# Float32 scores in the first two attention units, and VectorE takes five of eight low parts in the second MoE

## The chip, the cores and the metric

One core of a Trainium2 chip runs the whole program in one launch. The metric is the device time of that launch in microseconds (us). TensorE (PE, with its weight loads as PEld), VectorE (DVE), ScalarE (ACT), GpSimd (POOL) and SyncE (SP, which here issues every DMA) run side by side, each through its own instructions in order, and meet only at semaphores.

## The reference, cut to what matters

```python
def _attn_ref(q, k, v, tau):          # q, k, v: (4, 8, 576, 64), float32
    scores = scale * np.matmul(q, k.transpose(0, 1, 3, 2))
    thresh = np.max(scores, axis=-1, keepdims=True) - tau
    scores = np.where(scores >= thresh, scores, -1000000000.0)
    attn = np.exp(scores - np.max(scores, axis=-1, keepdims=True))
    attn = attn / (np.sum(attn, axis=-1, keepdims=True) + 1e-09)
    return np.matmul(attn, v)

def _moe_ref(x, w_in, w_out):         # x: (2304, 512), w_in: (512, 2048), w_out: (2048, 512)
    h = x @ w_in
    return (h * np.clip(h + 3.0, 0.0, 6.0) / 6.0) @ w_out

def _moe2_ref(x, w_in, w_out):
    h = x @ w_in
    return (h * (1.0 / (1.0 + np.exp(-1.702 * h)))) @ w_out

# x = attention, heads side by side; x = _moe_ref(x); result = _moe2_ref(x)
```

## The kernel before

**Products.** A float32 operand is written as a high part, rounded to the type float32r, and a low part, the rest. A product is then two or three float32r matmuls (high times high, high times low, low times high) that add up in PSUM. Nearly every operand so costs a copy on ACT, which makes the high part, and a subtraction on POOL or DVE, which makes the low part.

**Attention.** There are 16 units of two heads (function `unit`, numbers `u` from 0, four for each batch). For each head SP loads k and q from DRAM, where the host has put each of them twice, on rows 0 to 63 and again on rows 64 to 127. ACT copies k to `kh` and POOL subtracts to get `kl`; POOL scales q by 0.125, ACT copies it to `qs`, and POOL replaces rows 64 to 127 of `qs` by q's low part (L489 to L496). One matmul over 128 rows then gives (high of q + low of q) times `kh`, and a second one the same times `kl`: two for each half of the 576 keys, so four float32r matmuls of 288 columns for a score tile of 128 queries (L518 to L520). A unit has nine score tiles; the middle one holds the last 64 queries of both heads and takes two groups, so a unit has ten groups of four. Behind a score tile come DVE's maximum (`nm`, L529) and threshold, ACT's Exp (L531), DVE's mask with the sum (L532), the transposes on PE (L580), their copies to `eh`, and the product with v (L643 in the first four units, which use float32 there). Two PSUM buffers (`ps`) hold score tiles.

**First MoE.** Weights come as words of 64 bits and are decoded on ACT, DVE and POOL (`decode`, L397 to L399 on DVE); 16 weight tiles are decoded while the first units run. The first MoE of a batch starts when its four units have been turned into x (`moe_a`, L708 and L728), and fills PE between the later units.

**Second MoE** (from about 740 us of the span). Tokens go in five blocks (four of 512, one of 256), the hidden units in two halves, and each half in four pairs of 128 units: 10 blocks of 8 gated units, 80 in all. `hidden2` makes a pair's two sums in PSUM (L865) and brings them to `c` with DVE additions and ACT copies; `gate2` then does, for each of the two: sigmoid on ACT (`tc`, L846), product on DVE (`tc<-tc,c`), high part `g` on ACT, low part `g` on POOL (L849, in the trace at the helper's line L346). `yout` multiplies both parts with the output weights (L728, into `py`).

**What sets the order.** Every instruction is an operation of a plan with a cost and a due time. `Plan.settle` orders all of it by a list schedule (a forward pass by priority and backward passes that make the priorities anew) and the program is emitted in that order. A change of one cost or engine so moves many rows. The plan keeps names listed in `PORT` from running on DVE and POOL together; the low parts of a gate (`GL`) stand there for both engines.

Of the kernel before, what the change touches and what calls it, by code (L numbers as in the profile page):

```python
# [15 lines left out]
ALU = mybir.AluOpType  # L16
# [226 lines left out]
def tile_top_attention_moe_moe2(  # L243
# [21 lines left out]
    CH = [(0, 256), (256, 320)]  # L265
    FULL = 4
    scale = 0.125
# [59 lines left out]
    def pe(n):  # L327
        return 7 + 0.43 * n
# [10 lines left out]
    def pool2(n):  # L339
        return 149 + 2.1 * n  # L340
# [122 lines left out]
    def unit(u, b, j, t0):  # L463

        early = u < FULL
        slots, pad = [(0, 0), (1, 0), None, (0, 1), (1, 1)], 64
# [9 lines left out]
        for hd in range(2):  # L478
            h, q0 = 2 * j + hd, pad * hd
            s0 = min(n for n, t in enumerate(tiles) if t is None or t[0] == hd)  # L480
            kr, qr = (buf("qk", 3, "raw", [P, S]) for _ in range(2))
            khb, klb, qsb = (buf(x, 3, "st", [P, n], F32R) for x, n in (("kh", S), ("kl", S), ("qs", S + pad)))
            kh.append(khb), kl.append(klb), qs.append(qsb)
            cols = slice(q0, q0 + S)
            move(K("ld", s0), "ldk", 4 * P * S, lambda kr=kr, h=h: nc.sync.dma_start(out=kr.t, in_=k2[b, h]), [], [kr])

            for o, i, n in ((0, 256, 64), (64, 0, 256), (320, 320, 256)) if b == 0 and hd else ((0, 0, S),):
                move(K("ld", s0), "ldq", 4 * P * n, lambda qr=qr, h=h, o=o, i=i, n=n: nc.sync.dma_start(out=qr.t[:, o:o + n], in_=q2[b, h, :, i:i + n]), [], [(qr, o)])
# [21 lines left out]
        def score(s):  # L510
# [5 lines left out]

            def mm(hd, q0, st, sp):
                for w, a, z in ((kh, st, False), (kl, False, sp)):  # L518
                    for i in range(2):
                        nc.tensor.matmul(ps.t[:, i, :SH], qs[hd].t[:, q0:q0 + P], w[hd].t[:, i * SH:(i + 1) * SH], start=a, stop=z)  # L520

            for hd in range(2) if t is None else t[:1]:
                q0 = t[1] * P + 2 * pad * hd if t else 0 if hd else 512
                add(PE, 4 * pe(SH), K("S", s), "S", lambda hd=hd, q0=q0: mm(hd, q0, t is not None or hd == 0, t is not None or hd == 1), [qs[hd], kh[hd], kl[hd]], [ps])

# [312 lines left out]

    def gate2(c, T, K):
        t = buf("tc", 2, "ct", [P, 512])  # L840
# [11 lines left out]
    def hidden2(n, w, xs, whole, K):  # L852

# [27 lines left out]
        if whole:  # L881
# [4 lines left out]
            plus(b, first(b), bd, p1, 0)  # L886
            return [gate2(c, T, K) for c in (a, b)]
        p5, u2, bb = buf("p5", 1, "ct", [P, 256]), buf("u2", 1, "ct", [P, 256]), bank(3)
# [11 lines left out]
        add(ACT, act(n), K("H2") + 5000, "KP", copy(first(b), first(ba)), [ba], [(b, 0)])  # L900
        return [gate2(c, T, K) for c in (a, b)]

    def moe2(c0, T, f0, w, t0, last):
# [18 lines left out]
        for i in range(len(w)):  # L922
            g2 = hidden2(n, w[i], xs, whole, lambda name, i=i: K(name, i))
            if i:
                yout(i - 1, gs)
            gs = g2
        yout(len(w) - 1, gs)
        for c in range(KC):
# [15 lines left out]
            else:  # L944
# [116 lines left out]
```

## Time and profile before

| | us |
|---|---|
| median of 3 runs | 1147.12 (1145.11 to 1147.84) |
| the profiled execution | 1150.94 |
| its span, first to last instruction | 1149.2 |
| PE busy in it | 1094.7 (95%) |
| DVE / ACT / POOL busy in it | 785.2 / 705.1 / 705.3 |
| mean granted TensorE clock | 0.994 |

A matmul counts as busy until its result has drained, so a PE that is busy 95% of the time is not one that streams columns 95% of the time; how dense it is shows in the starts of its instructions. The difference between the profiled execution and the median is that of single executions, and sums are made against the profiled one.

### The profile page before, as it was taken

Reading aid. Unit: us, or ns where it says so; the run is one execution under the profiler, and the core shown is the slowest. Engines: PE = TensorE matmul, PEld = TensorE weight load, DVE = VectorE, ACT = ScalarE, POOL = GpSimd, SP = SyncE. Lnnn points to the kernel's source line nnn. Section 1 sums busy time; section 2 is a strip of 40 time slices with the busy share of each in tenths; the row PEclk is TensorE's granted clock in tenths of the full one; section 3 lists DMA queues with packets and bytes.
Section 4 is the critical chain, followed back from the end, with each engine's and each line's share of the span. In section 5 each row is a group of like instructions: output and inputs, shape, how many; then the busy total and the mean of one; then the engine's idle time right before and its main releaser. Section 6 shows DMA issues by size and latency. Waiting matters only on the chain.

```text
span 1149.2 us, 21102 instructions
## 1 busy us (share of the span) xinstructions
PE 1094.7 (95%) x7560; PEld 1005.9 (88%) x7560; DVE 785.2 (68%) x1596; ACT 705.1 (61%) x1452; POOL 705.3 (61%) x738
## 2 busy tenths in 40 slices
PE   4999999999999999999899999989999999999998
PEld 3655799989999999999899999988888888889788
DVE  5978886989599959767876432686677865543423
ACT  6877976778678867666554333655556565444432
POOL 6768898878688976556566224675564665432421
PEclk9999999999999999999999999999999999999999
DMA  6434322222222220145664312432544435312202
GB/s 187 149 114 128 98 63 68 75 76 74 67 77 79 69 67 28 48 148 165 194 185 133 98 55 71 152 110 77 172 132 166 157 114 166 111 37 74 88 1 69
DMA packets 79752, 119.00 MB, mean 104 GB/s; under 512 B 7840, under 2 KB 50464, under 8 KB 79648
## 3 DMA queue, kind: packets, MB, share of 16 engines
q1 hardware_dynamic: 79648, 117.67, 33.3%
q8 instruction: 59, 0.97, 0.4%
q14 instruction: 45, 0.37, 0.1%
HBM read 87.10 MB, written 30.54 MB: 102 GB/s over the span
## 4 chain that ended last, share of the span: by engine, by line
PE 60%; DVE 14%; issue 9%; POOL 7%; ACT 6%; DMA 5%; SPq 0%; POOLq 0%; DVEq 0%; ACTq 0%
PE py L728 15%; PE pm L708 14%; PE pm L865 8%; PE pm L728 5%; PE ps L520 5%; PE pm L580 5%; PE pm L643 4%; DVE nm L529 2%; POOL g L346 2%; PE pm L645 2%; DVE e L532 2%; PE pm L647 1%; DVE tc L346 1%; DVE el L346 1%; DVE outlring L346 1%
## 5 line engine op out<-in xcount | busy, mean ns | idle before, releaser
L728 PE MATMUL py<-g,outhring 128*128 128x512 f32 (+2 forms) x1152 | 291.2, 338 | 12.0 <-POOL g L346 8.5
L728 PEld LDWEIGHTS py<-g,outhring 128*128 128x128 f32 x1152 | 193.7, 188 | 35.1 <-POOL g L346 14.1
L346 POOL TENSOR_TENSOR g<-tc,g 128x512 fp32r<-128x512 f32 (+1 forms) x80 | 101.5, 1273 | 158.9 <-ACT g L343 136.9
L728 PE MATMUL py<-g,outlring 128*128 128x512 f32 (+2 forms) x576 | 193.6, 336 | 0.0
L865 PE MATMUL pm<-outhring,inhring 128*128 128x256 f32 x512 | 146.0, 285 | 8.6 <-ACT p L343 4.1
L708 PE MATMUL pm<-xh,inhring 128*128 128x256 f32 (+1 forms) x512 | 153.2, 299 | 0.8 <-DVE t L720 0.3
L708 PE MATMUL pm<-xl,inhring 128*128 128x256 f32 (+1 forms) x512 | 151.2, 295 | 0.0
L708 PE MATMUL pm<-xh,inlring 128*128 128x256 f32 (+1 forms) x512 | 151.0, 295 | 0.0
L865 PE MATMUL pm<-outlring,inhring 128*128 128x256 f32 x512 | 144.0, 281 | 0.0
L865 PE MATMUL pm<-outhring,inlring 128*128 128x256 f32 x512 | 143.8, 281 | 0.0
L346 POOL TENSOR_TENSOR g<-t,g 128x256 fp32r<-128x256 f32 (+1 forms) x104 | 85.7, 828 | 92.2 <-ACT g L343 89.3
L529 DVE TENSOR_REDUCE nm<-ps 128x1 f32<-128x576 f32 x144 | 107.7, 752 | 24.1 <-PE ps L520 23.0
L720 DVE SCALAR_TENSOR_TENSOR t<-t,pm 128x256 f32<-128x256 f32 (+1 forms) x128 | 57.3, 450 | 93.8 <-ACT t L719 93.3
L343 ACT ACTIVATE eh<-pm 128x512 fp32r<-128x512 f32 (+9 forms) x240 | 108.2, 486 | 19.7 <-PE pm L580 18.3
L728 PEld LDWEIGHTS py<-g,outlring 128*128 128x128 f32 x576 | 108.2, 188 | 9.8
L728 PE MATMUL pm<-g,outhring 128*128 128x256 f32 (+1 forms) x512 | 109.4, 303 | 2.1 <-DVE g L346 1.0
L865 PEld LDWEIGHTS pm<-outhring,inhring 128*128 128x128 f32 x512 | 96.8, 189 | 15.4 <-ACT p L343 5.3
L719 ACT ACTIVATE t<-pm,half 128x256 f32<-128x256 f32 (+1 forms) x128 | 63.6, 497 | 75.9 <-PE pm L708 70.0
L531 ACT ACTIVATE e<-ps,nm 128x576 f32<-128x576 f32 x128 | 93.8, 738 | 22.9 <-DVE nm L529 20.1
L532 DVE SCALAR_TENSOR_TENSOR e<-ps,th,e 128x576 f32<-128x576 f32 x128 | 103.0, 811 | 6.4 <-ACT e L531 4.9
L580 PE MATMUL pm<-id,e 128*128 128x128 f32 (+1 forms) x640 | 98.2, 278 | 7.7 <-DVE e L532 7.1
L865 PEld LDWEIGHTS pm<-outlring,inhring 128*128 128x128 f32 x512 | 97.0, 189 | 2.7
(115 smaller groups left out, 2856.1 us busy)
## 6 DMA issues: line engine op xcount, KB each, us to landing
qk<-in_k_dram SPq DMA_DIRECT2D x32, 288.0 KB, 2.9
wrawstg<-in_w1i_dram SPq DMA_DIRECT2D x16, 512.0 KB, 3.8
wrawstg<-in_w1o_dram SPq DMA_DIRECT2D x16, 512.0 KB, 3.5
wrawstg<-in_w2i_dram SPq DMA_DIRECT2D x16, 512.0 KB, 3.8
wrawstg<-in_w2o_dram SPq DMA_DIRECT2D x16, 512.0 KB, 3.7
qk<-in_q_dram SPq DMA_DIRECT2D x28, 288.0 KB, 2.8
wrawstg<-kept SPq DMA_DIRECT2D x20, 256.0 KB, 3.7
xa<-x2d SPq DMA_DIRECT2D x8, 512.0 KB, 3.8
```

The costliest lines, as they stand in the source:

```text
L343: return lambda: nc.scalar.activation(out=o(), in_=i(), func=ACTF.Copy, **kw)
L346: return lambda: (nc.vector if eng == DVE else nc.gpsimd).tensor_tensor(out=o(), in0=a(), in1=b(), op=op)
L520: nc.tensor.matmul(ps.t[:, i, :SH], qs[hd].t[:, q0:q0 + P], w[hd].t[:, i * SH:(i + 1) * SH], start=a, stop=z)
L529: add(DVE, 665, K("R", s), "R", lambda: nc.vector.tensor_reduce(out=nm.t[:, c], in_=ps.t[:, :, :SH], op=ALU.max, axis=AX.XY, negate=True), ...
L531: add(ACT, 624, K("X", s), "X", lambda: nc.scalar.activation(out=ev(), in_=ps.t[:, :, :SH], func=ACTF.Exp, bias=nm.t[:, c]), [ps, (nm, s)] ...
L532: add(DVE, 729, K("M", s), "M", lambda: nc.vector.scalar_tensor_tensor(out=ev(), in0=ps.t[:, :, :SH], scalar=th.t[:, c], in1=ev(), op0=ALU ...
L580: nc.tensor.transpose(pt.t[:kn, o + m * P:o + (m + 1) * P], e_of[s].t[:, ks], id_b.t)
L708: nc.tensor.matmul(ph.t[:, :n], a, v, start=(cc == 0 and i == 0), stop=(cc == KC - 1 and i == 2))
L719: add(ACT, 93 + act(n), K("RL"), "RL", lambda: nc.scalar.activation(out=tt_(), in_=pt(), func=ACTF.Relu, scale=1.0 / 6.0, bias=half_b.t), ...
L720: add(DVE, dve(n), K("GT"), "GT", lambda: nc.vector.scalar_tensor_tensor(out=tt_(), in0=tt_(), scalar=1.0, in1=pt(), op0=ALU.min, op1=ALU. ...
L728: nc.tensor.matmul(py.t[:, :n], a, v, start=(st and i == 0), stop=(sp and i == 2))
L865: nc.tensor.matmul(o.t[:, :n], u.t[:, ws], v.t[:, xv], start=(st and kk == 0 and i == 0), stop=(sp and kk == 1 and i == 2), skip_group_che ...
```

## The change

In units 0 and 1 (`EXACT = 2`) the score operands stay float32: q and k are loaded on rows 0 to 63 only, straight into `qs` and `kh`, POOL fills the other rows with zeros, and DVE scales q in place. The four float32r matmuls of a group become two float32 matmuls. The copies to `kh` and `qs`, the subtractions for `kl` and q's low part and POOL's scaling go away for these four heads. In the second MoE DVE, not POOL, makes the low part of the second gated unit of each pair, and of both units of the last pair of a block: 50 of 80.

```diff
-    FULL = 4
+    FULL, EXACT = 4, 2
...
+            pieces = ((0, 256, 64), (64, 0, 256), (320, 320, 256)) if b == 0 and hd else ((0, 0, S),)
+            if exact:
+                add(POOL, 124 + 0.52 * (S + pad), K("qz", s0), "qz", lambda qsb=qsb: nc.gpsimd.memset(f32(qsb.t)[64:], 0.0), [], [(qsb, 1)])
+                add(POOL, 100, K("qz", s0), "qz", lambda qsb=qsb, z=(1 - hd) * S: nc.gpsimd.memset(f32(qsb.t)[:64, z:z + pad], 0.0), [], [(qsb, 2)])
+                add(POOL, 124 + 0.52 * S, K("qz", s0), "qz", lambda khb=khb: nc.gpsimd.memset(f32(khb.t)[64:], 0.0), [], [(khb, 1)])
+                for o, i, n in pieces:
+                    move(K("ld", s0), "ldq", 256 * n, lambda qsb=qsb, h=h, o=q0 + o, i=i, n=n: nc.sync.dma_start(out=f32(qsb.t)[:64, o:o + n], in_=q2[b, h, :64, i:i + n]), [], [(qsb, o)])
+                move(K("ld", s0), "ldk", 256 * S, lambda khb=khb, h=h: nc.sync.dma_start(out=f32(khb.t)[:64], in_=k2[b, h, :64]), [], [(khb, 0)])
+                for o, i, n in pieces:
+                    add(DVE, 69 + 0.521 * n, K("qs", s0), "qs",
+                        lambda qsb=qsb, c=slice(q0 + o, q0 + o + n): nc.vector.tensor_scalar(out=f32(qsb.t)[:64, c], in0=f32(qsb.t)[:64, c], scalar1=sc_b.t[:64], scalar2=1.0, op0=ALU.mult, op1=ALU.mult), [sc_b], [(qsb, o)])
+                continue
...
             def mm(hd, q0, st, sp):
+                if exact:
+                    for i in range(2):
+                        nc.tensor.matmul(ps.t[:, i, :SH], f32(qs[hd].t)[:, q0:q0 + P], f32(kh[hd].t)[:, i * SH:(i + 1) * SH], start=st, stop=sp)
+                    return
...
-        add(POOL, pool2(T), K("GL2"), "GL", tt(POOL, v(gl), v(t), lambda: f32(v(gh)()), ALU.subtract), [t, gh], [gl])
+        add(eng, pool2(T) if eng == POOL else dve(T), K("GL2"), "GL", tt(eng, v(gl), v(t), lambda: f32(v(gh)()), ALU.subtract), [t, gh], [gl])
...
-            g2 = hidden2(n, w[i], xs, whole, lambda name, i=i: K(name, i))
+            g2 = hidden2(n, w[i], xs, whole, lambda name, i=i: K(name, i), (DVE, DVE) if i == len(w) - 1 else (POOL, DVE))
```

How the order moves is shown at three places.

POOL at the start of the program, before the change, from behind the first fills (`kl` and the second `qs` are the low parts of k and q, `qk` is raw k or q):

```order
L496 MEMSET qs 128x64
L365 MEMSET two 64x64 x2
L346 ISA
L346 TENSOR_TENSOR kl<-qk,kh 128x576
L492 TENSOR_SCALAR qk<-qk,sc 128x576
L346 TENSOR_TENSOR kl<-qk,kh 128x576
L346 TENSOR_TENSOR qs<-qk,qs 64x576
L346 TENSOR_TENSOR id_107<-id 128x64
```

The same place of the changed program:

```order
L488 MEMSET qs 64x640
L489 MEMSET qs 64x64
L490 MEMSET kh 64x576
L488 MEMSET qs 64x640
L489 MEMSET qs 64x64
L490 MEMSET kh 64x576
L365 MEMSET two 128x128
```

Four long operations that the first scores need have gone from POOL; fills of zeros, which wait for no load, stand there instead.

PE at the start, before (`ps` score tiles, `pm<-id,e` transposes, `pm<-eh,vs` products with v; a group of four score matmuls is two rows `kh` and two rows `kl` of a half each, printed as pairs):

```order
L520 MATMUL ps<-kh,qs 128x288 x2
L520 MATMUL ps<-kl,qs 128x288 x2
L520 MATMUL ps<-kh,qs 128x288 x2
L520 MATMUL ps<-kl,qs 128x288 x2
L580 MATMUL pm<-id,e 128x128 x8
L580 MATMUL pm<-id,e 64x128 x2
L520 MATMUL ps<-kh,qs 128x288 x2
L520 MATMUL ps<-kl,qs 128x288 x2
```

And in the changed program:

```order
L535 MATMUL ps<-kh,qs 128x288 x6
L599 MATMUL pm<-id,e 128x128 x8
L599 MATMUL pm<-id,e 64x128 x2
L535 MATMUL ps<-kh,qs 128x288 x2
L662 MATMUL pm<-eh,vs 64x256 x5
```

A score group is one row of two matmuls, and three groups, no longer two, stand ahead of the first transposes.

DVE at the end of the last block of 512 tokens in the second MoE, before (`c` the sums, `tc` the gate, `yc` the output):

```order
L346 TENSOR_TENSOR c<-pm,p_14137 128x256
L346 TENSOR_TENSOR c<-pm,u_14189 128x256
L346 TENSOR_TENSOR c<-pm,p_14147 128x256
L346 TENSOR_TENSOR tc<-tc,c 128x512 x2
L346 TENSOR_TENSOR yc<-py_13982,yc 128x512
```

And in the changed program:

```order
L346 TENSOR_TENSOR c<-pm,u_14119 128x256
L346 TENSOR_TENSOR g<-tc,g 128x512
L346 TENSOR_TENSOR tc<-tc,c 128x512
L346 TENSOR_TENSOR g<-tc,g 128x512
L346 TENSOR_TENSOR c<-pm,p_14098 128x256
L346 TENSOR_TENSOR tc<-tc,c 128x512
L346 TENSOR_TENSOR g<-tc,g 128x512
L346 TENSOR_TENSOR yc<-py_13924,yc 128x512
```

The low parts `g<-tc,g` now stand between the products and the sums on DVE; the sums and the outputs queue behind them.

## Rows read from the trace of the kernel before

**Rows 1.** The head of the page.

```profile
span 1149.2 us, 21102 instructions
```

**Rows 2.** Windows: stretch, length; busy us PE, PEld, DVE, ACT, POOL; clock; DMA.

```profile
10.46:65.00 54.54, 48.55 (x258) 34.05 (x258) 46.12 (x104) 45.51 (x89) 40.46 (x47) 0.97 0.47 141
...
740.00:1149.00 409.00, 388.47 (x2478) 346.69 (x2476) 238.31 (x358) 209.23 (x436) 197.26 (x149) 1.00 0.33 106
```

**Rows 3.** Timeline, start to first MoE matmul: start, length, instruction, idle before.

```profile
0.72 0.38 SPq L485 DMA_DIRECT2D qk<-in_k_dram  x1
...
2.09 0.43 SPq L485 DMA_DIRECT2D qk<-in_k_dram  x1
...
3.60 0.68 ACT L343 ACTIVATE kh<-qk 128x576 fp32r<-128x576 f32 x1 [1.61 <-DMA qk<-in_k_dram]
...
6.77 0.68 ACT L343 ACTIVATE kh<-qk 128x576 fp32r<-128x576 f32 x1 [2.49 <-DMA qk<-in_k_dram]
...
9.01 1.39 POOL L346 TENSOR_TENSOR qs<-qk,qs 64x576 fp32r<-64x576 f32 x1
...
10.46 0.85 PE L520 MATMUL ps<-kh,qs 128*128 128x288 f32 x2 [10.46 <-POOL qs L346]
...
124.07 0.28 PE L708 MATMUL pm<-xh,inhring 128*128 128x256 f32 x1
```

**Rows 4.** Timeline of PE alone: float32r pairs, then float32 products (two records each).

```profile
23.19 0.43 PE L520 MATMUL ps<-kh,qs 128*128 128x288 f32 x2
23.45 0.42 PE L520 MATMUL ps<-kl,qs 128*128 128x288 f32 x2
...
34.17 1.83 PE L643 MATMUL pm<-eh,vs 128*64 128x320 f32 x6
...
39.79 1.29 PE L643 MATMUL pm<-eh,vs 128*64 128x320 f32 x4
```

**Rows 5.** Waits of 10 to 124 us: us in total, times, longest.

```profile
DVE nm L529 <- PE ps L520: 16.2, 18, 2.5
```

**Rows 6.** The chain that ended last, 10 to 60 us, by line.

```profile
by line: PE pm L643 35.0%; PE ps L520 28.4%; PE pm L580 18.8%; DVE nm L529 5.9%; issue 4.2%; DVE e L532 3.6%; POOL qs L346 2.8%; DVE th L530 1.2%; PE pm L571 0.9%; DVE wmstg L397 0.7%; DVE er L532 0.5%; DVE rc L539 0.2%; DVE wmstg L399 0.1%
```

**Rows 7.** Groups by form, 10.46 to 65 us: busy us, mean ns, idle before.

```profile
L397 DVE TENSOR_SCALAR wmstg<-wmstg 128x512 f32<-128x512 f32 x6 | 5.0, 834 | 6.7 <-ACT wmstg L396 6.7
...
L346 POOL TENSOR_TENSOR qs<-qk,qs 64x576 fp32r<-64x576 f32 x5 | 7.1, 1428 | 1.7 <-ACT qs L343 1.3
L346 POOL TENSOR_TENSOR kl<-qk,kh 128x576 fp32r<-128x576 f32 x5 | 7.1, 1420 | 1.1 <-ACT kh L343 1.0
L492 POOL TENSOR_SCALAR qk<-qk,sc 128x576 f32<-128x576 f32 x6 | 4.8, 805 | 4.1 <-DMA qk<-in_q_dram 4.0
```

**Rows 8.** Waits of PE, 740 to 1149 us.

```profile
PE py L728 <- POOL g L346: 8.5, 13, 1.6
...
PE pm L865 <- DVE c L346: 2.3, 4, 1.0
```

**Rows 9.** Groups by form, 740 to 1149 us.

```profile
L346 DVE TENSOR_TENSOR tc<-tc,c 128x512 f32<-128x512 f32 x64 | 60.1, 939 | 38.5 <-ACT tc L846 37.8
...
L346 POOL TENSOR_TENSOR g<-tc,g 128x512 fp32r<-128x512 f32 x64 | 88.6, 1386 | 133.7 <-ACT g L343 111.8 <-issue 9.3 <-PE pm L865 6.4
```

**Rows 10.** DVE on the tile tc, 740 to 1149 us: ns min/median/max.

```profile
L346 DVE TENSOR_TENSOR tc<-tc,c x80: 410/692/1808, 742.4 to 1140.9; 128x512 f32<-128x512 f32 x64, 128x256 f32<-128x256 f32 x16
```

**Rows 11.** Timeline at the end of a block of the second MoE.

```profile
1069.30 1.31 POOL L346 TENSOR_TENSOR outlring<-xb,outhring 128x512 fp32r<-128x512 f32 x1 [0.55 <-ACT outhring L343]
...
1069.55 1.61 DVE L346 TENSOR_TENSOR tc<-tc,c 128x512 f32<-128x512 f32 x1
...
1075.56 1.30 POOL L346 TENSOR_TENSOR outlring<-xa,outhring 128x512 fp32r<-128x512 f32 x1 [2.32 <-ACT outhring L343]
...
1076.82 1.26 POOL L346 TENSOR_TENSOR g<-tc,g 128x512 fp32r<-128x512 f32 x1
1078.13 0.50 PE L728 MATMUL py<-g,outhring 128*128 128x512 f32 x1 [1.58 <-POOL g L346]
```

More of the change, by code (lines that the diff above doesn't have):

```diff
@@ L463, in unit @@
     def unit(u, b, j, t0):
-        early = u < FULL
+        early, exact = u < FULL, u < EXACT
         slots, pad = [(0, 0), (1, 0), None, (0, 1), (1, 1)], 64
@@ L480, in unit @@
             s0 = min(n for n, t in enumerate(tiles) if t is None or t[0] == hd)
+            khb, qsb = (buf(x, 3, "st", [P, n], F32R) for x, n in (("kh", S), ("qs", S + pad)))
+            kh.append(khb), qs.append(qsb)
+            cols = slice(q0, q0 + S)
+            pieces = ((0, 256, 64), (64, 0, 256), (320, 320, 256)) if b == 0 and hd else ((0, 0, S),)
[10 more added lines that the diff above has]
+                continue
             kr, qr = (buf("qk", 3, "raw", [P, S]) for _ in range(2))
-            khb, klb, qsb = (buf(x, 3, "st", [P, n], F32R) for x, n in (("kh", S), ("kl", S), ("qs", S + pad)))
-            kh.append(khb), kl.append(klb), qs.append(qsb)
-            cols = slice(q0, q0 + S)
+            klb = buf("kl", 3, "st", [P, S], F32R)
+            kl.append(klb)
             move(K("ld", s0), "ldk", 4 * P * S, lambda kr=kr, h=h: nc.sync.dma_start(out=kr.t, in_=k2[b, h]), [], [kr])
-            for o, i, n in ((0, 256, 64), (64, 0, 256), (320, 320, 256)) if b == 0 and hd else ((0, 0, S),):
+            for o, i, n in pieces:
                 move(K("ld", s0), "ldq", 4 * P * n, lambda qr=qr, h=h, o=o, i=i, n=n: nc.sync.dma_start(out=qr.t[:, o:o + n], in_=q2[b, h, :, i:i + n]), [], [(qr, o)])
@@ L523, in score @@
                 q0 = t[1] * P + 2 * pad * hd if t else 0 if hd else 512
-                add(PE, 4 * pe(SH), K("S", s), "S", lambda hd=hd, q0=q0: mm(hd, q0, t is not None or hd == 0, t is not None or hd == 1), [qs[hd], kh[hd], kl[hd]], [ps])
+                add(PE, (8 if exact else 4) * pe(SH), K("S", s), "S", lambda hd=hd, q0=q0: mm(hd, q0, t is not None or hd == 0, t is not None or hd == 1), [qs[hd], kh[hd]] + ([] if exact else [kl[hd]]), [ps])
             def ev():
@@ L837, in halves, with gate2 @@
         return out_
-    def gate2(c, T, K):
+    def gate2(c, T, K, eng):
         t = buf("tc", 2, "ct", [P, 512])
@@ L848, in gate2, with hidden2 @@
         add(ACT, 42 + act(T), K("GH2"), "GH", copy(v(gh), v(t)), [t], [gh])
-        add(POOL, pool2(T), K("GL2"), "GL", tt(POOL, v(gl), v(t), lambda: f32(v(gh)()), ALU.subtract), [t, gh], [gl])
+        add(eng, pool2(T) if eng == POOL else dve(T), K("GL2"), "GL", tt(eng, v(gl), v(t), lambda: f32(v(gh)()), ALU.subtract), [t, gh], [gl])
         return gh, gl
-    def hidden2(n, w, xs, whole, K):
+    def hidden2(n, w, xs, whole, K, engs):
         a, b = (buf("c", 3, "ct", [P, 512]) for _ in range(2))
@@ L886, in hidden2 @@
             plus(b, first(b), bd, p1, 0)
-            return [gate2(c, T, K) for c in (a, b)]
+            return [gate2(c, T, K, eng) for c, eng in zip((a, b), engs)]
         p5, u2, bb = buf("p5", 1, "ct", [P, 256]), buf("u2", 1, "ct", [P, 256]), bank(3)
@@ L900, in hidden2 @@
         add(ACT, act(n), K("H2") + 5000, "KP", copy(first(b), first(ba)), [ba], [(b, 0)])
-        return [gate2(c, T, K) for c in (a, b)]
+        return [gate2(c, T, K, eng) for c, eng in zip((a, b), engs)]
     def moe2(c0, T, f0, w, t0, last):
@@ L946, in moe2 @@
             move(t, "SO", 4 * P * T, lambda o=o, rows=rows: nc.sync.dma_start(out=(out if last else y2d)[rows, c0:c0 + T], in_=o()), [yc], [] if last else [y2d_b[c0]])
-    NOMINAL = dict(ld=-20000, ldv=-16000, kh=-9000, kl=-8500, qs=-8200, qh=-8000, ql=-7500, vh=-1000, vl=-800, S=0, R=600, TH=1400, X=1400, M=2200, GD=2900, RC=3000, N=3200,
+    NOMINAL = dict(ld=-20000, ldv=-16000, qz=-8300, kh=-9000, kl=-8500, qs=-8200, qh=-8000, ql=-7500, vh=-1000, vl=-800, S=0, R=600, TH=1400, X=1400, M=2200, GD=2900, RC=3000, N=3200,
                    T=5000, EF=5400, EH=5500, EL=6000, AV=7000, RB=8500, BT=9000, XR=9400, XM=9600, XH=10000, XL=10500, ST=10000, H=0, RL=1500, GT=2000, GH=2500, GL=3000,
```

## Prediction

> **What bounds the kernel now.** I read the head of the page, the windows by stage, PE's waits in each stage, and then the timeline at the two places that the change touches. The span is 1149.2 us [rows 1], 1.7 us less than the execution's own 1150.94. PE does nothing for the first 10.46 us [rows 3], and most of the rest it is busy: between 740 us and the end 388.5 of 409 us, while DVE is busy for 238 and POOL for 197 [rows 2]. So the kernel ends when PE has done its work, plus PE's holes. There are three sorts of hole that matter here.
>
> The first is the start. The first load of k is issued at 0.72 us and has landed when ACT copies it at 3.60; from there a row of copies and subtractions runs, and the last of them, POOL's low part of q, starts at 9.01 and lasts 1.39, so that PE starts at 10.46, released by it [rows 3].
>
> The second is the first units, up to the first matmul of the first MoE at 124.07 us [rows 3], where no MoE work can fill in. Between 10.46 and 65 us DVE is busy 46.1 of 54.5 us, PE 48.6, ACT 45.5, POOL 40.5 [rows 2]: nobody is full, and they wait for each other in turn. The reader should see both sides of it: the chain goes through PE for 83% (35.0 + 28.4 + 18.8 + 0.9) [rows 6], and DVE's maxima waited 16.2 us in 18 places for a score tile [rows 5].
>
> The third is in the second MoE: PE waits 8.5 us in 13 places for POOL's low part of the gate, more than for DVE's sums, 2.3 [rows 8].
>
> **The change: the start.** Gone from the path are two copies, two subtractions and the scaling on POOL. What is left is load, scaling on DVE, matmul. The order has tau, q and k as the first three loads. If each lands as the first one did, 2.9 us from issue (0.72 to 3.60 [rows 3]), and the third is issued at about 1.6 us, k is there at 4.5. DVE's scaling of 576 columns is not in the trace; the nearest row is its scaling of 512 columns, a mean of 834 ns in which other work held it up [rows 7], and that is the upper bound; it starts when q is there, one issue before k, so it is hidden for at least half. PE then starts at about 5.0. The other end: the second load of k, issued at 2.09, was used at 6.77, 4.7 us later [rows 3], which gives 1.6 + 4.7 + 0.2 = 6.5. The new fills of zeros wait for nothing and are over before a load lands. I take 5.0: **-5.5 us**, bounds -4.0 and -5.5.
>
> **Float32 scores.** A float32r matmul of 288 columns comes every 0.13 us (a pair at 23.19, the next at 23.45), so a group of four takes 0.52 [rows 4]. Float32 scores are not in the trace, but float32 products with v are: three of them on 320 columns (six records) take 1.83 us, two take 1.29, so one takes 0.54, or 0.486 for 288 columns [rows 4]. A group of two is 0.97, which is 0.45 more; with the tail left in (1.83 / 3 = 0.61, so 0.55) it would be 0.58 more. Two units have 20 groups: PE gets 20 x 0.45 = 9.0 us more work, at most 11.6.
>
> The Trainium skill (FP8 and Floating Point Precision, TensorE Precision Notes) says that true float32 takes four passes through the array. By it a matmul would cost 4 x 0.13 = 0.52, a group 0.52 more and the 20 groups 10.4 us, a sum that would come out 0.7 us higher; it lies between my two readings, and I keep the row's.
>
> How much of the 9.0 lies on the path? If PE's holes in the first units hid all of it, nothing; by the chain [rows 6] 83%, 7.5 us; all of it at worst. Against it stands relief: POOL loses four times 1.42 + 1.43 + 0.81 us [rows 7], 14.6 of its 40.5 us in that stretch. DVE gets four scalings, 4 x 0.83 = 3.3 us at most. And the score groups of the second head no longer wait for their low part. I take half, **+4.5 us**, with the bounds 0 and 9.0. The copies that ACT loses (kh, 0.68 each [rows 3], and qs) I count at nothing, since ACT is not full and PE's chain covers them; if ACT does become the last to come, this is a small gain.
>
> **Low parts on DVE.** POOL takes 1386 ns for a low part of 512 columns [rows 9]. DVE has not done this one here; the nearest row is its product `tc<-tc,c` of the same shape, also with both inputs in SBUF: 692 ns at the median [rows 10], 939 in the mean [rows 9]. So a low part is ready 0.69 us earlier at best and 0.45 earlier in the mean; and where POOL was not free, more: at the block's end POOL began the low part at 1076.82, behind another operation of 1.30 us, and PE stood for 1.58 us [rows 11]. The 13 waits have a mean of 0.65 us [rows 8]. With 0.45 each I get 13 x 0.45 = 5.9, with 0.69 all 8.5; I take **-6.5 us**, bounds 0 (another operation is the last to come) and -8.5. Forty of the 50 are of 512 columns: DVE gets at most 50 x 0.94 = 47 us on top of 238 in 409 us [rows 2, 9], 70% busy. It is still no bound, but what is queued behind a low part on DVE are the sums `c`, which free PSUM banks for PE.
>
> **The sum.** -5.5 + 4.5 - 6.5 = -7.5 us: 1143.4 for an execution like the profiled one. The median lies 3.8 below it, so 1147.1 - 7.5 = **1139.6 us**. Everything between 124 and 740 us is put in a new order by the same rules, without new work; I count it at nothing and give it 3 us to either side. Half of a PE that runs full there hides no PE work, so what is won ahead of it stays won.
>
> **The rivals.**
> 1. *The holes hide the float32 work.* The holes that the units leave on PE, and less work on POOL, speak for it; the chain speaks against it. -5.5 - 6.5 = -12.0: 1135.1 us.
> 2. *PE pays all of it.* The chain's 83% and DVE's waits for score tiles speak for it, the four engines that take turns against it. -5.5 + 9.0 - 6.5 = -3.0: 1144.1 us; with the dearer reading (11.6) 1146.7.
> 3. *The wait in the second MoE only changes its name.* PE would wait for ACT's high part or its copies instead. For it: POOL waits 111.8 us for ACT's `g` [rows 9], so ACT comes just ahead. Against it: where PE stood longest, POOL was the last by a whole operation [rows 11]. The first two terms alone, -1.0: 1146.1 us.
> 4. *Slower: DVE's low parts are held up by POOL and hold up the sums.* At 1069.55 a DVE product took 1.61 us and not 0.69 while POOL worked from 1069.30 on [rows 11]: 0.92 us lost. If each of the 50 low parts makes PE wait 0.3 us, that is +15 on the -7.5: 1154.6 us. It turns the sign from 7.5 / 50 = 0.15 us each. Against it: DVE's median is its undisturbed time [rows 10], so most of its products were not held, and POOL has 50 operations fewer that could hold one.
>
> The Trainium skill (SBUF — State Buffer, Who interferes with whom) states this lock as a rule: a DVE instruction with two SBUF inputs and a GpSimd instruction that reads SBUF exclude each other, and the later one blocks fully. The 1.61 us agree. By the rule alone the price depends on how often they meet, and the rows' mean says about a third of the time.
>
> **How the numbers follow.** About 0.3%, 3.4 us, is what a measurement of this kernel can tell from no change. Forecast 0.41; rival 1 0.18; rival 2 0.17; rival 3 0.12; rival 4 0.12. Of the forecast's 0.41 I give 0.06 to a gain under 3.4 us; of rival 2, at 3.0 us, 0.07 to a gain over it; rival 3's gain is too small to tell. Faster: 0.35 + 0.18 + 0.07 + 0.02 for the order in between, 0.62. Same: 0.26. Slower: 0.12. The range reaches from rival 1 with a little more from the new order, 1133, to rival 3 and the dear rival 2 with some of the same against it, 1148; rival 4 and a gain in all three places stay outside.
>
> **What would show it.** PE's first matmul at 4.5 to 6.5 us, released by DVE's scaling or k's load. Score groups that start 0.97 us apart when they follow each other. The first matmul of the first MoE at 122 to 125 us; by 118 for rival 1, 127 or later for rival 2. In the second MoE PE's waits for a low part, POOL's and DVE's together, at 1 to 3 us and no longer 8.5, and its waits for DVE's sums still under 5; these above 10 would be rival 4, and those for ACT's `g` above 5 rival 3. The forecast falls if the score groups cost more than 1.1 us, or if the middle stretch, 124 to 740 us, gives or takes more than 3 us by its order alone.

## The result

The changed kernel takes 1128.74 us (median of 4 runs, 1127.03 to 1129.64), the kernel before 1146.11 us (1143.23 to 1147.84) in the same set. The ratio is 0.9855, 95% interval 0.9833 to 0.9878. The gain of 17 us is more than twice the forecast of 7.5, and the time lies below the forecast's range (1133 to 1148). A second set (e5 below) gave 0.9849. The profiled execution took 1127.03 us, 23.9 less than that of before; 4.8 us of this are that the profiled execution of before lay above the median of this set, and 1.7 that the new one lies below its own.

The head of the page, changed kernel [rows 1]:

```profile
span 1125.2 us, 21023 instructions
```

Windows of the changed kernel, columns as in [rows 2]; the first is the stretch from PE's first matmul to 65 us, the last the second MoE:

```profile
4.96:65.00 60.04, 56.45 (x268) 36.42 (x269) 50.52 (x124) 46.93 (x91) 39.15 (x49) 1.00 0.55 164
...
740.00:1125.00 385.00, 370.62 (x2373) 333.33 (x2371) 241.47 (x383) 198.09 (x407) 133.01 (x94) 1.00 0.34 110
```

POOL has 133 us of work in the second MoE and no longer 197, and DVE is busy for 63% of that stretch (58% before). In the first stretch POOL is busy for 65% and no longer for 74%.

The timeline of the changed kernel: the start, then the first matmuls of the first and of the second MoE, with what stands ahead of them [rows 3]:

```profile
1.17 0.56 SPq L492 DMA_DIRECT2D qs<-in_q_dram  x1
...
1.78 0.58 SPq L493 DMA_DIRECT2D kh<-in_k_dram  x1
...
3.94 0.83 DVE L496 TENSOR_SCALAR qs<-qs,sc 64x576 f32<-64x576 f32 x1 [0.70 <-DMA qs<-in_q_dram]
...
4.96 4.16 PE L535 MATMUL ps<-kh,qs 128*128 128x288 f32 x8 [4.96 <-DMA kh<-in_k_dram]
...
111.77 0.39 PE L727 MATMUL pm<-xh,inhring 128*128 128x256 f32 x1
...
722.56 0.28 PE L884 MATMUL pm<-outhring,inhring 128*128 128x256 f32 x1
```

PE starts 5.50 us earlier, released by k's load 0.2 us after DVE's scaling has ended. The first MoE begins 12.3 us earlier; 6.8 us of that were won after the start, in part because the new order puts fewer matmuls ahead of it (520 records, before 536) and because the clock did not fall there (see the end). The second MoE begins 13.8 us earlier (before: 736.40 in the same view) and is 10.2 us shorter (722.56 to 1125.2, against 736.40 to 1149.2).

A row of three float32 score groups in PE's timeline, and the next instruction (four records for a group; [rows 4]):

```profile
42.08 3.08 PE L535 MATMUL ps<-kh,qs 128*128 128x288 f32 x12
45.09 0.75 PE L662 MATMUL pm<-eh,vs 64*64 64x320 f32 x2
```

45.09 - 42.08 = 3.01 us, and 3.01 / 3 = 1.00 us for a group, where the prediction had 0.97 from the row of float32 products. The Trainium skill (FP8 and Floating Point Precision, TensorE Precision Notes) has four passes for true float32. With the 0.13 us of [rows 4] this makes an estimate of 1.04; the measured value lies between the two.

DVE's waits for score tiles from 10 to 124 us, 16.2 us before [rows 5], are halved (L535 is units 0 and 1, L539 the units behind):

```profile
DVE nm L548 <- PE ps L539: 4.5, 6, 1.5
DVE nm L548 <- PE ps L535: 3.9, 5, 1.2
```

PE's waits in the second MoE [rows 8], from 720 us on:

```profile
PE py L747 <- DVE g L346: 4.4, 4, 1.7
PE pm L884 <- DVE c L346: 3.0, 4, 1.2
PE py L747 <- POOL g L346: 2.6, 4, 1.3
PE pm L884 <- ACT p L343: 1.3, 1, 1.3
PE pm L884 <- ACT u L343: 1.0, 1, 1.0
```

Waits for low parts are still 7.0 us. What has gone besides is waits for ACT's copies of the sums, which before stood in the same view from 737 us on:

```profile
PE pm L865 <- ACT p L343: 4.1, 5, 1.2
PE pm L865 <- ACT u L343: 2.0, 4, 0.6
```

PE's waits fall from 17.3 us in all to 12.3, half of what the stage is shorter by. The waits of the weight loads (PEld) tell more; first before, then the changed kernel, over the same stretches:

```profile
PEld py L728 <- POOL g L346: 13.9, 18, 1.9
PEld pm L865 <- ACT p L343: 5.3, 6, 1.4
PEld pm L865 <- DVE c L346: 4.5, 9, 1.2
PEld pm L865 <- ACT u L343: 2.8, 4, 0.8
PEld py L728 <- ACT g L343: 2.2, 6, 0.6
...
PEld py L747 <- DVE g L346: 8.5, 12, 1.9
PEld pm L884 <- DVE c L346: 4.1, 4, 1.4
PEld py L747 <- POOL g L346: 3.7, 4, 1.6
PEld pm L884 <- ACT p L343: 1.7, 2, 1.5
PEld pm L884 <- ACT u L343: 1.2, 1, 1.2
```

They fall from 28.7 us to 19.2. Of these 9.5 us only 1.7 are low parts; 5.2 are ACT's copies of the sums, 2.2 ACT's high parts and 0.4 DVE's sums.

And the low parts themselves, tile `g` on DVE and on POOL (ns min/median/max):

```profile
L346 DVE TENSOR_TENSOR g<-tc,g x50: 415/692/1784, 731.3 to 1118.4; 128x512 fp32r<-128x512 f32 x40, 128x256 fp32r<-128x256 f32 x10
...
L346 POOL TENSOR_TENSOR g<-tc,g x30: 733/1297/2195, 729.5 to 1115.2; 128x512 fp32r<-128x512 f32 x24, 128x256 fp32r<-128x256 f32 x6
```

DVE's median is the 692 ns of its product [rows 10].

### The profile page after: what moved, and what is told of

It is laid out like the page before. It is cut to its first block, busy times and chain, and to the rows that moved or that the text cites. A ratio compares the mean times of both kernels' runs of the same rounds, so it can differ in the third digit from the quotient of the medians.

```text
span 1125.2 us, 21023 instructions
## 1 busy us (share of the span) xinstructions
PE 1091.7 (97%) x7560; PEld 1005.3 (89%) x7560; DVE 797.0 (71%) x1654; ACT 703.6 (63%) x1444; POOL 640.5 (57%) x684
## 4 chain that ended last, share of the span: by engine, by line
PE 68%; DVE 14%; ACT 6%; POOL 4%; DMA 4%; issue 4%; SPq 1%; POOLq 0%; DVEq 0%; ACTq 0%
PE py L747 19%; PE pm L727 14%; PE pm L884 12%; PE pm L747 7%; PE pm L599 4%; PE ps L539 4%; PE pm L662 3%; DVE e L551 2%; DVE nm L548 2%; PE pm L664 2%; PE pm L666 1%; DVE el L346 1%; DVE g L346 1%; PE ps L535 1%; DVE tc L346 1%
## 5 line engine op out<-in xcount | busy, mean ns | idle before, releaser
L346 POOL TENSOR_TENSOR g<-tc,g 128x512 fp32r<-128x512 f32 (+1 forms) x30 | 39.5, 1316 | 140.8 <-ACT g L343 89.5
L548 DVE TENSOR_REDUCE nm<-ps 128x1 f32<-128x576 f32 x144 | 107.5, 752 | 16.9 <-PE ps L539 10.2
L346 POOL TENSOR_TENSOR wmstg<-wmstg,wrstg 128x512 uint32<-128x512 uint32 x48 | 66.2, 1380 | 61.3 <-DVE wmstg L399 36.8
L727 PEld LDWEIGHTS pm<-xh,inhring 128*128 128x128 f32 x512 | 96.9, 189 | 2.6 <-PE pm L599 0.7
```

The lines of the kernel that those rows point to most:

```text
L346: return lambda: (nc.vector if eng == DVE else nc.gpsimd).tensor_tensor(out=o(), in0=a(), in1=b(), op=op)
L548: add(DVE, 665, K("R", s), "R", lambda: nc.vector.tensor_reduce(out=nm.t[:, c], in_=ps.t[:, :, :SH], op=ALU.max, axis=AX.XY, negate=True), ...
L727: nc.tensor.matmul(ph.t[:, :n], a, v, start=(cc == 0 and i == 0), stop=(cc == KC - 1 and i == 2))
```

## The experiments

Four numbers are read from each profile: PE's first matmul; the first matmul of the second MoE; the **way** between the two, which holds all of attention and the first MoE; and the length of the second MoE, from its first matmul to the end of the span. The last column is the time before the second MoE in which the granted clock stood at one half (see the end). Ratios are to the kernel before in the same set, with 95% intervals; single executions of one kernel differ by some 4 us. Each execution's mean granted clock was measured too; what it is short of 1, times the span, is called the time **lost to the clock** below, a mean over the executions of a run.

| kernel | median us | ratio | first | 2nd MoE | way | length | half clock |
|---|---|---|---|---|---|---|---|
| before (profile) | 1147.12 | | 10.46 | 736.40 | 725.9 | 412.8 | 13.7 |
| after (profile) | 1128.74 | 0.9855 (0.9833 to 0.9878) | 4.96 | 722.56 | 717.6 | 402.6 | 3.4 |
| e1 scores alone | 1141.56 | 0.9956 (0.9940 to 0.9972) | 4.87 | 725.24 | 720.4 | 411.4 | 3.4 |
| e2 low parts alone | 1141.04 | 0.9940 (0.9920 to 0.9960) | 10.27 | 734.02 | 723.8 | 402.9 | 10.2 |
| e3 scores twice, before | 1151.99 | 1.0039 (1.0025 to 1.0053) | 9.99 | 736.71 | 726.7 | 414.1 | 3.4 |
| e4 POOL's work back | 1145.53 | 0.9977 (0.9961 to 0.9994) | 8.39 | 742.58 | 734.2 | 401.9 | 13.7 |
| e5 after again | 1131.45 | 0.9849 (0.9828 to 0.9870) | 4.87 | 725.21 | 720.3 | 403.4 | 6.8 |
| e6 no low parts, before | 1147.99 | 0.9995 (0.9977 to 1.0013) | 6.86 | 732.92 | 726.1 | 412.8 | 6.8 |
| e7 after, other order | 1139.43 | 0.9913 (0.9887 to 0.9939) | 4.90 | 737.39 | 732.5 | 403.5 | 10.2 |
| e8 before, other order | 1148.99 | 1.0002 (0.9982 to 1.0022) | 10.16 | 735.84 | 725.7 | 412.5 | 6.8 |
| e9 after, 2 passes | 1137.81 | 0.9902 (0.9869 to 0.9935) | 5.00 | 732.64 | 727.6 | 403.8 | 6.8 |
| e10 after, 4 passes | 1137.11 | 0.9899 (0.9868 to 0.9931) | 4.96 | 730.09 | 725.1 | 404.7 | 0 |
| e11 before, 2 passes | 1149.81 | 1.0013 (0.9989 to 1.0036) | 10.87 | 729.18 | 718.3 | 415.8 | 0 |
| e12 before, 4 passes | 1151.10 | 1.0021 (1.0002 to 1.0039) | 9.95 | 736.15 | 726.2 | 411.7 | 10.2 |
| e13 after in before's order | 1133.42 | 0.9863 (0.9836 to 0.9890) | 5.39 | 731.09 | 725.7 | 401.0 | 13.7 |
| e14 before in after's order | 1154.94 | 1.0055 (1.0035 to 1.0075) | 9.57 | 735.25 | 725.7 | 419.7 | 10.2 |
| e15 last pair alone | 1134.71 | 0.9880 (0.9856 to 0.9903) | 4.96 | 724.93 | 720.0 | 406.0 | 6.8 |
| e16 alternating alone | 1132.76 | 0.9866 (0.9833 to 0.9898) | 4.87 | 722.52 | 717.6 | 405.2 | 3.4 |
| e17 POOL's work back, after's order | 1140.04 | 0.9940 (0.9922 to 0.9959) | 8.69 | 734.85 | 726.2 | 403.4 | 6.8 |
| e18 no low parts, before's order | 1141.71 | 0.9957 (0.9940 to 0.9973) | 7.21 | 725.72 | 718.5 | 412.5 | 0 |

**The two halves, and the whole again.** e1 is the changed kernel with the low parts back on POOL, e2 with float32r scores, e5 the changed kernel itself.

```diff
-... (DVE, DVE) if i == len(w) - 1 else (POOL, DVE))
+... (POOL, POOL))                        # e1
-    FULL, EXACT = 4, 2
+    FULL, EXACT = 4, 0                   # e2
```

> Float32 scores in units 0 and 1 alone; all gate low parts stay on POOL. The changed kernel's trace starts the first MoE at 111.8 us (before 124.1) and the second MoE 13.8 us earlier than before, of which 5.5 us are the earlier start. My prediction's term for this half was -1.0 us, that is 1145 us. Theory 'relief' (POOL, ACT and so the weight decode are freed in the first units) and theory 'clock' (a denser PE has no half-clock stretches in the first 124 us; before had three, at 54, 81 and 109 us) both expect some -10 to -13 us, 1133 to 1136 us, with the first MoE at 110 to 114 us. Theory 'order' (the list schedule of this one program happened to come out well, and another program with the same scores need not) allows anything from 1133 to 1143, with the first MoE between 112 and 122 us.

> The low parts on DVE alone; all units keep float32r scores. The second MoE of the changed kernel took 402.6 us, before 412.8. My prediction's term was -6.5 us: 1139.6 us. If the two halves of the change add up, this one is 1146.1 - 17.4 + what the scores alone gain, so 1136 to 1139 us with a second MoE of 401 to 405 us and the first MoE at 124 us as before. If the second MoE gained only because it met another order (theory 'order'), 1140 to 1146 us.

> The changed kernel again, unaltered, beside the others on one chip. The two halves alone gave ratios of 0.9956 and 0.994, 0.9896 together, and the whole change 0.9855 in another set of runs. If the halves add up, 0.989 to 0.991 here, 1134 to 1136 us; if there is more in the pair than in its halves (their orders differ), 0.985 again, 1129 us.

Each half gains, 5.0 and 6.9 us by the ratio. They show apart in the trace: only e1 has the early start, only e2 the short second MoE. Together they make 12 of the 17 us. Of e1's 5.0 us 2.0 are the clock (2.5 us lost to it, 4.5 before).

**How much added PE work is hidden.** e3 is the kernel before with every score group of units 0 and 1 issued twice, the second time over the first result in PSUM, so that the scores stay the same: 10.4 us more PE work and nothing else.

```diff
+                for r in range(2):   # three times and once for the two groups of the middle tile
                     for w, a, z in ((kh, st, False), (kl, False, sp or r < 1)):
```

> The kernel before with the score matmuls of units 0 and 1 issued twice (the second time over the first result, so that the output stays the same): 20 x 0.52 = 10.4 us more PE work in the first units, nothing freed on POOL, ACT or DVE, no earlier start. Theory 'clock' expects that a denser PE keeps its clock: none of the half-clock stretches between 20 and 65 us, the first MoE at 122 to 127 us, 1144 to 1149 us. Theory 'relief' expects that PE work without relief is paid, first MoE at 129 to 134 us, 1151 to 1156 us. If 'relief' and 'clock' both count, something between.

It costs 4.5 us by the ratio (5.6 if the time lost to the clock, 3.4 us and 4.5 before, is taken off): something near half, the factor that the prediction took, in a sequence that the plan made for it.

**POOL's relief, with sequences of their own.** e4 puts a subtraction, a scaling and a subtraction on POOL, on the rows of zeros, ahead of each of the four float32 heads. e6 takes the same sort of work out of the kernel before: the low parts of q and k are left out in units 0 and 1 (float32r scores of high parts alone, `kh` used twice), and DVE scales q.

```diff
+                add(POOL, 1360, K("kl", s0), "kl", tt(POOL, kh[64:], kh[64:], qs[64:, :S], ALU.subtract), ...)     # e4
+                add(POOL, pool1(S), K("qs", s0), "qs", tensor_scalar(qs[64:, :S] times 1.0), ...)
+                add(POOL, pool2(S), K("ql", s0), "ql", tt(POOL, qs[64:, :S], qs[64:, :S], kh[64:], ALU.subtract), ...)
```

> The changed kernel with the POOL work that it removed put back: per float32 head two subtractions and a scaling over 576 columns, on the rows of zeros, which stay zero (the output stays the same); they wait for no load, but the scores wait for them. POOL gets its 4 x 3.65 = 14.6 us back; the start may come up to 3.5 us later, to be taken out by counting from the first score. From the first score to the first MoE the kernel before took 113.6 us, the changed one 106.8. Theory 'relief' expects 111 to 115 us again, 1134 to 1140 us in all. Theory 'clock' expects 106 to 109 us, no half-clock stretch, and no more than the late start's 0 to 3.5 us: 1129 to 1132 us.

> The kernel before with units 0 and 1 freed of POOL's three operations a head and nothing else of the change: four float32r matmuls a group as before (kh twice, with q scaled by half), loads and ACT copies as before, scaling on DVE, zeros in rows 64 to 127 of qs. The low parts of q and k in these two units are left out, so their scores are float32r ones. Theory 'relief' (POOL's 14.6 us hold up the first units and the weight decode) expects a gain larger than the changed kernel's first half, since the float32 passes are not paid: 10 to 16 us, 1131 to 1137 us, with a start at 6 to 7.5 us. If relief is worth no more than the start, 3 to 4 us, 1143 us.

They contradict each other: the work put back costs 14 to 17 us, the work taken out gains nothing. Both had been given a new sequence, so neither tells what POOL's work is worth.

**Other sequences.** The list schedule's priorities are kicked at random once (e7, e8), or it makes two or four backward passes for three (e9 to e12). The instructions are the same, their order differs.

```diff
-KICKS = ()
+KICKS = (1,)                 # e7 of after, e8 of before
-        for _ in range(3):
+        for _ in range(2):       # e9 of after, e11 of before; range(4): e10 of after, e12 of before
```

> The changed kernel with one random disturbance of the priorities ahead of the last two passes of the list schedule: the same instructions in another order. Theory 'order' expects a change of the size of the unexplained part, 5 to 10 us, in either direction. If the order is worth as little as I took it, at most 3 us.

> The kernel before with the same disturbance of its priorities. Theory 'order': 5 to 10 us in either direction. Otherwise at most 3 us.

> The changed kernel ordered with two backward passes and not three: the same instructions, another order. The chosen order reaches the second MoE at 722.6 to 725.2 us of the span, the randomly disturbed one at 737.4, the kernel before at 734.0 to 736.4. Theory 'order' (what went beyond the earlier start is this order's luck): the second MoE begins anywhere from 724 to 740 us, mean near 730 (the start's 5.5 us). Theory 'scores' (float32 scores as such make the first units shorter): 722 to 728 us, and the disturbed order was a bad one.

> The changed kernel with four backward passes. As for two passes: 'order' allows 724 to 740 us for the start of the second MoE, 'scores' 722 to 728 us.

> The kernel before with two backward passes. The spread of its own orders: so far the second MoE begins at 734.0 to 736.4 us in its own order and at 735.8 in the disturbed one. 'order' expects that some order of the kernel before is as good as the changed kernel's, 726 to 745 us over these runs; 'scores' expects 732 to 740 us, none under 730.

> The kernel before with four backward passes. 'order': 726 to 745 us for the start of the second MoE; 'scores': 732 to 740 us.

The sequence is worth more than the 3 us that the prediction gave it: the changed kernel loses 6 to 8 us against e5 in all three, and still gains 0.9 to 1.0% on before; the kernel before loses nothing, 1.5 and 2.4 us by the ratio. The clock is not the reason: e7, e9 and e10 lose 4.3, 2.3 and 1.5 us to it, e5 3.2. The length of the second MoE hardly cares: 403.5 to 404.7 with low parts on DVE, 411.7 to 415.8 without.

**The sequences exchanged.** The start times that the plan gave each operation of the one kernel serve as priorities for the other, instead of the passes. TensorE then runs nearly the sequence of the other kernel.

```diff
-        for _ in range(3):
-            key = self.latest()
-            length = self.order(key)
+        self.order(start times of the other kernel's plan, by operation)
```

> The changed program, with the sequence of the kernel before as its priorities (PE then runs nearly the sequence of before; the low parts stay on VectorE, the scores float32). Theory 'order': most of what the changed kernel gains ahead of the second MoE is its sequence. The second MoE then starts at 729 to 735 us, not at 722.6 to 725.2, its length stays 402 to 405, and the median is 1136 to 1141. Rival 'float32 scores': fewer operations ahead of each score are worth the same in any sequence. The second MoE starts at 722 to 726 and the median stays at 1129 to 1132.

> The kernel before, with the sequence of the changed one as its priorities (float32r scores with all their copies and subtractions, low parts on POOL). 'Order': the second MoE starts at 727 to 731 us, not at 734 to 736.4, its length is 411 to 416, the median 1138 to 1142. 'Float32 scores': a sequence made without the copies doesn't suit a kernel that has them; the second MoE starts at 734 or later, the median is 1146 or more.

e13 is the cleanest comparison of the study. In before's own sequence the changed kernel gains 1.4% (15.7 us by the ratio). Its median is 2 to 5 us above that of the changed kernel in its own sequence, and the intervals of the two ratios overlap; e13 loses 5.9 us to the clock, the changed kernel 2.0 and 3.2 (e5), so that the clock alone makes 3 to 4 us of this. PE has some 9 to 10 us more to do in the way (20 groups of 1.00 for 0.52), and the way is as long as before, 725.7 against 725.9, with 13.7 us at half clock in both. By its times and not by its place in the sequence, then, the float32 work found room.

It found it late. Up to the first matmul of the first MoE, with the same 536 records on PE in both, e13 needs 118.7 us (5.39 to 124.05) and before 113.6, each with 10.2 us at half clock: 5.1 us of the added work are paid there. From there to the second MoE e13 needs 607.0 us, before 612.3, with 3.4 us at half clock each and nothing changed in the work: what was paid comes back. About 2.6 us of it come back by 224 us, which no run explains. The other 2.7 are one event in the profile of before, a hole on PE with a fall of the clock (241.8, see the end); e2, which has before's sequence there, has neither and stands 2.7 us further ahead behind it. Against e2's way of 723.8 us e13's is 1.9 longer. So the float32 work cost 0 to 2 us by the second MoE.

The bounds set for it in advance split: the place of the second MoE (731.1) and the median (1133.4, between the two forecasts) side with 'order' in the first and with neither in the second. e14 is plain, and falls to the side of 'float32 scores': the new sequence does nothing for a kernel that still makes copies and low parts, and its second MoE is 6.9 us longer (the clock fell twice in it, up to 3.4 us of this).

**POOL's relief, with the sequence held.** e4 and e6 again, e17 in the order of the changed kernel and e18 in that of before.

> The changed program with POOL's 14.6 us of work on the first four heads put back (as in e4), and with the sequence of the changed kernel as its priorities, which e4 did not have. Theory 'POOL's relief hides the float32 work': PE waits for late operands whatever the sequence; the second MoE starts at 734 us or later and the median is 1140 to 1147. Rival 'sequence': e4 lost its 14 us to the sequence that the plan made for it; here only the later start is lost, the second MoE starts at 725 to 731 and the median is 1132 to 1138.

> The kernel before without the low parts of q and k in the first four heads (as in e6: float32r scores of half the precision, ACT's copies stay, POOL's 14.6 us are gone), with the sequence of the kernel before as its priorities, which e6 did not have. 'POOL's relief': PE's holes shrink as in e13, the second MoE starts at 722 to 729 us, the median is 1135 to 1141. 'Sequence': e6 had nothing to gain, and here only the earlier start shows; second MoE at 731 to 734, median 1143 to 1147.

POOL's work put back makes the way 5.9 to 8.6 us longer (726.2 against 717.6 and 720.3), besides a start that is 3.7 later; 8.6 to 11.3 us by the medians. Taken out of the kernel before, it makes the way 7.4 us shorter and the start 3.3 earlier; 0.43% by the ratio, 5 us. By the bounds that is relief's side in both, at the edge of its range in e17's median and 0.7 us over it in e18's. For e17 it stands: it loses as much to the clock as e5 (3.0 and 3.2 us), both profiles have 6.8 us at half clock, and the way is 5.9 us longer. For e18 it does not stand by itself. The clock never fell in its way, and fell for 13.7 us in that of before, which is worth up to 6.8 of the 7.4 us; over all executions e18 loses 2.4 us to the clock and before 4.7, and these 2.3 us with the start's 3.3 are all that it gains (5.2 us in the means).

**Which low parts count.** e15 gives DVE only the last pair of each block, e16 one of every pair.

```diff
-... (DVE, DVE) if i == len(w) - 1 else (POOL, DVE))
+... (DVE, DVE) if i == len(w) - 1 else (POOL, POOL))     # e15
+... (POOL, DVE))                                         # e16
```

> The changed program, but with VectorE taking the low parts of the last pair of each block alone (20 of 80), POOL all others. Theory 'block end': the second MoE is shorter because PE no longer stands at the end of a block for the last low part. Its length is 403 to 406 us. Rival 'each its share': each low part that moves saves the same, 9.4 us for 50, so 20 save 3.8 and the length is 408 to 410.

> The changed program, but with VectorE taking the second low part of every pair, the last one too (40 of 80). 'Block end': POOL and VectorE share the last pair, so part of the wait is gone; length 405 to 409 us. 'Each its share': 40 save 7.5, length 404 to 406.

Twenty low parts at the block ends shorten the second MoE to 406.0, from 411.4 in e1; forty spread over the pairs bring 405.2. So not each has its share: the last pair is worth more than half of the whole. It may be nearly all: in e15 the clock fell twice within the second MoE (at 753.3 and 930.8), up to 3.4 us of its 406.0, in e16 once (750.1), in e1, e5 and the changed kernel not before the end. But PE's waits in e15 from 720 us on are not what 'block end' had in mind:

```profile
PE py L747 <- DVE g L346: 4.8, 5, 2.0
PE py L747 <- ACT g L343: 3.6, 3, 2.3
PE py L747 <- POOL g L346: 1.5, 3, 1.1
PE pm L884 <- ACT p L343: 1.8, 2, 1.0
PE pm L884 <- ACT u L343: 0.3, 1, 0.3
```

The waits of `py` for a gate add up to 9.9 us, no less than before; the waits of `pm` for a free bank of sums are down to 2.1, before 8.4. The weight loads' waits (18.6 us in e15, 27.3 in e1) follow the length again: in the eight profiles of before, after, e1, e2, e5, e13, e15 and e16 the length, less these waits and half of the time at half clock in it, is 382.4 to 384.1 us.

## Why the prediction was wrong

**The start** was right: -5.50 us by the trace, -5.5 forecast; k's load took 3.2 us from issue to use, 2.9 forecast.

**The size of the float32 scores** was right: 1.00 us a group, 0.97 forecast, the four-pass reading 1.04.

**The step that failed is "I take half, +4.5 us, with the bounds 0 and 9.0", and with it "what is won ahead of it stays won".** With the sequence of before on PE (e13) a half is about right where the first MoE begins, 5.1 us; but it does not stay. 5.3 us come back before the second MoE, and of the 9 to 10 us 0 to 2 are left on the path, the lower bound and rival 1's case. In the changed kernel's own sequence the way is even 5.6 to 8.3 us shorter than before, 3.4 to 5.1 of this at most by the clock. The factor a half is what added work costs in the end when nothing is taken off the other engines (e3), and the prediction used it although it had listed what is taken off: POOL's 14.6 us, ACT's copies, the second head's wait for its low part. e17 prices POOL's relief with the sequence held: 5.9 to 8.6 us of the way. That this alone hid the float32 work is not shown: e18 gained nothing by it beyond the start and the clock, and what ACT's copies do was not tried alone. DVE's maxima, which waited 16.2 us for score tiles, wait 8.4, and PE, which stood 7.1 us for DVE's masks ahead of its transposes from 10 to 124 us, shows no such wait in the changed kernel; but in e13 5.1 of the 7.1 us are still there, so this is not what hid the work there.

```profile
PE pm L580 <- DVE e L532: 7.1, 5, 2.3
...
PE pm L784 <- DVE e L736: 5.1, 5, 1.9
```

Rival 1 gave 1135.1 us; e13 measured 1133.4, with rival 1's nothing for the scores and more for the low parts. The chain's 83%, on which the path share was argued, said where time ended, not that PE was full there: I now read it as a PE that kept coming late by its operands, which is a reading and was not tested.

**The low parts** were under-sized: -6.5 forecast, and the second MoE is 8.0 to 10.2 us shorter (e5 against e1, after against before; e2's ratio alone is worth 6.9). The price of one was right (692 ns). Its effect was misread. Waits for low parts were to fall from 8.5 us to 1 to 3 and fell to 7.0 only; waits for ACT's copies of the sums, which the prediction had not counted, went from 6.1 to 2.3, and in the waits of the weight loads, which the prediction did not read, the copies count for three times as much as the low parts (5.2 and 1.7 us). Rival 3, that PE would wait for ACT instead, is refuted, and so is rival 4: waits for DVE's sums are 3.0 us, and DVE's low parts have the undisturbed median. Why ACT's copies come earlier is not settled; less on POOL and a new order of ACT came together in every run.

**"Everything between 124 and 740 us is put in a new order ... I count it at nothing and give it 3 us to either side"** was too narrow. From the first matmul of the first MoE to that of the second the changed kernel needs 610.8 us, before 612.3, so the step held for this sequence. It doesn't hold as a bound: in before's sequence (e13) it takes 607.0, and in the changed kernel's three other sequences 615.1 to 615.6 us, over 4 us more by order alone, and the first units before it are up to 10 us later. That its own sequence is better than that of before is not shown: its median is 2 to 5 us lower, of which the clock makes 3 to 4.

By the runs, then: -5.5 for the start, 0 to +2 for the scores, -8 to -10 for the low parts, -2 to -5 for the clock and the order together, which makes -13.5 to -20.5 for the measured 17. The prediction had no term for the clock.

## What to carry to other kernels

When a change puts work on the engine at the bound and takes some off engines that feed it, price the two together: the work taken off can open less waiting than the chain shows, or, as here, room for nearly all of the added work, and far behind the place where it was added. Where a list schedule sets the order, any edit draws a new sequence, and that draw alone moved this kernel by up to 8 us; hold the sequence (the other kernel's start times as priorities) before calling an edit good or bad. A wait named in a list is no fixed sum to be won: the last pair's low parts shortened the second MoE by more than half of the gain while the waits for gates stayed. Read the weight loads' waits beside PE's: here they, and not PE's, followed the length of the stage.

## What the runs showed of the hardware

A hole on PE can cost more than itself. In PE's timeline of the kernel before, a hole of 1.72 us ends at 53.44, and a little later float32r pairs and products with v come more slowly; nine products take 3.62 us, where ten of the same shape take 2.52 at full clock (19.45 in the last rows of this section):

```profile
53.44 0.55 PE L580 MATMUL pm<-id,e 128*128 128x128 f32 x3 [1.72 <-DVE e L532]
53.74 0.58 PE L520 MATMUL ps<-kh,qs 128*128 128x288 f32 x2
54.11 0.68 PE L520 MATMUL ps<-kl,qs 128*128 128x288 f32 x2
54.73 3.62 PE L643 MATMUL pm<-eh,vs 128*64 128x256 f32 x9
```

The windows of the kernel before show the granted clock there, and at the three other places ahead of the second MoE, at half, which is 1.2 of 2.4 GHz:

```profile
54.00:57.40 3.40, 3.40 (x11) 1.95 (x11) 3.18 (x7) 2.37 (x4) 2.94 (x6) 0.51 0.78 255
81.30:84.70 3.40, 3.23 (x9) 1.93 (x10) 3.37 (x6) 2.00 (x5) 2.80 (x3) 0.51 0.41 107
108.60:112.00 3.40, 3.40 (x9) 1.35 (x7) 3.36 (x6) 2.39 (x4) 2.64 (x3) 0.51 0.50 159
241.80:245.20 3.40, 3.21 (x14) 3.23 (x15) 2.83 (x10) 1.14 (x3) 3.13 (x5) 0.50 0.39 143
```

Holes of 1.72, 1.72, 1.93 and 1.24 us end ahead of the four or just within (at 53.44, 81.47, 107.40 and 240.93). The PE of e2 runs the same sequence around the last of them, without this hole and without the fall; between 237 and 246 us it gains 2.7 us on that of before, more than the hole. But not every hole brings a fall: in e17 one of 3.02 us ends at 15.91, and the clock stays full until 106.3. The changed kernel has one fall ahead of the second MoE, at 548.3, behind a wait of 1.26 us for a low part:

```profile
546.92 0.39 PE L747 MATMUL py<-g,outhring 128*128 128x256 f32 x1 [1.26 <-DVE g L346]
...
4.96:111.77 106.81, 100.86 (x520) 66.17 (x521) 89.18 (x213) 87.33 (x173) 78.83 (x92) 1.00 0.51 155
...
548.30:551.70 3.40, 3.40 (x18) 3.40 (x17) 2.35 (x5) 1.40 (x3) 2.03 (x2) 0.50 0.78 240
```

A stretch of 3.4 us at half the clock by itself costs at most 1.7 us, so the difference of 10.2 us in such time between the two profiles is worth up to 5.1 us of their 23.9. On float32 scores it shows plainly in PE's timeline of e13, where the clock is at half at first (two holes of 1.58 and 1.94 us end at 10.93 and 13.19) and full behind; the last two rows are windows with the granted clock:

```profile
10.93 0.33 PE L784 MATMUL pm<-id,e 128*128 128x128 f32 x1 [1.58 <-DVE e L736]
13.19 2.18 PE L784 MATMUL pm<-id,e 128*128 128x128 f32 x9 [1.94 <-DVE e L736]
15.50 4.02 PE L720 MATMUL ps<-kh,qs 128*128 128x288 f32 x8
19.45 2.52 PE L847 MATMUL pm<-eh,vs 128*64 128x256 f32 x10
21.89 3.18 PE L720 MATMUL ps<-kh,qs 128*128 128x288 f32 x12
24.91 0.27 PE L784 MATMUL pm<-id,e 128*128 128x128 f32 x1
...
12.40:19.20 6.80, 5.88 (x17) 4.22 (x17) 5.21 (x11) 2.23 (x6) 3.78 (x3) 0.50 0.90 240
20.00:30.00 10.00, 8.80 (x41) 5.68 (x39) 8.78 (x23) 7.73 (x14) 5.35 (x9) 1.00 0.34 103
```

A group takes 3.95 / 2 = 1.98 us at half the clock and 3.02 / 3 = 1.01 at full. How often the clock falls differs among executions, and that is most of their spread. Over the 84 executions of the kernel before that ran beside e1 to e18, the time lost to the clock is 0 to 10.4 us, 5.1 in the mean, and the execution's time rises by 0.95 us with each us of it; taking it off brings the standard deviation from 2.6 us to 1.4. The changed kernel's executions lose 2.0 us in the mean in the first set and 3.2 in e5's, where the kernel before loses 5.2. So about 2 us of the gain (16.1 us between the means of e5's set) are the clock, which falls less often in the changed kernel.
